# RWKV-7 attention and a cosine MoE on one core: r with v in block-diagonal products of two heads, memsets behind the first loads, and a new written order

## The chip, the core and the metric

The kernel runs on one core of a Trainium2 chip. The metric is the device time of one execution in microseconds. Before the change three runs gave 759.09, 759.76 and 762.46 us, a median of 759.76 us. A profiled execution of the same kernel took 755.39 us.

## The reference

The inputs r, k, v, w, a and b have the shape (4, 8, 768, 40): batch, heads, sequence, head size. The first part is a recurrence over the sequence with one 40x40 state for each of the 32 pairs of batch and head. The second part takes the result as 3072 tokens of 320 features through two weight matrices with a product with a cosine between them.

```python
for t in range(S):
    kt, vt, rt = (k[:, :, t], v[:, :, t], r[:, :, t])
    wt, at, bt = (w[:, :, t], a[:, :, t], b[:, :, t])
    y[:, :, t] = np.einsum('bhd,bhde->bhe', rt, state)
    Sa = np.einsum('bhde,bhe->bhd', state, at)
    state_decay = state * wt[:, :, None, :] - np.einsum('bhd,bhe->bhde', Sa, bt)
    state = state_decay + np.einsum('bhd,bhe->bhde', vt, kt)
...
h = x @ w_in
g = h * np.cos(h)
return (g @ w_out).astype(np.float32)
```

w_in is 320x2048 and w_out 2048x320; both arrive as 64-bit floats, which the kernel rounds to 32 bits by its own integer and float steps on VectorE and ScalarE.

## The kernel before

The sequence is cut into 24 chunks of 32 steps. Within a chunk the recurrence is solved with matrices: decays are multiplied up (w), a, b, k, r and v are brought into a layout with the features on the partitions, products between them give 32x32 matrices for each batch and head ("gram" is k with a and r with v; "nps" is b with a), a triangular inverse is computed on VectorE for four chunks at a time, and a chain of TensorE steps carries the state from chunk to chunk: t (turn the state), q (state with r), x, s, z. Every two chunks make a group of 256 tokens for the MoE: twelve groups, each in four parts j. A part is fa and fb (x with w_in, in the tile ph), y (cosine and product), then u, m, ms and c (the second product in the seven-product form; the first groups use the plain form sd).

The features of two heads (e = 0 and 1) lie in partitions 0 to 39 and 64 to 103; 40 to 63 and 104 to 127 are padding. A matrix product of one head therefore uses 40 rows of TensorE, and two heads use different halves of the rows. The output is 32 partitions for each of the four batches (blk, line 190).

The order of all instructions is a text, PLAN (line 17): 1536 tokens, which do() at line 532 executes one after the other; each engine, and each DMA queue, keeps that order for its own instructions. The tokens that are needed here:

- L:c:n:queue:part loads input n of chunk c (chunks 0 to 3), as two DMAs of 40 KB (load, line 256) from SyncE (s), ScalarE (a) or GpSimd (p). ld:c:n loads later chunks from SyncE.
- pw, pa, pb, pn (lines 538 to 637) make the turned w, a and b of two chunks and their products. pa calls over_w (line 563), whose reciprocal runs on VectorE and whose product bn on GpSimd reads nat_b; from_one (line 559) is a small memset of wb on GpSimd, and a_W (line 569) multiplies a by the decays on VectorE.
- sf, sc, ss (lines 344 to 367) fetch, multiply up and store w for later chunks; wf, wt, wm, wg, wp (line 413 on) round one piece of the weights; is, ip, ij, it, ih, ie, F and S make the inverse.
- in copies v and r of a chunk into vp and rp; v, k turn them with TensorE (chunks 0 to 7; from chunk 8 on r and v are turned through DRAM: rf, pt, st, and lt:c:n loads the turned tile, line 303).
- g is p2_g (line 759), with the two gram products; tk and tb take a chunk's result through DRAM into the MoE's input xT (line 938).
- B:n, K:n and P:n put n matmuls on the zero tile idle into TensorE's queue (lines 1150 to 1179).

Ahead of the plan stand constants and memsets: the identity (line 224), the mask su with its four selections (line 376), the paddings of seven tiles bn and two kn (lines 393 to 396), idle (line 406), all on GpSimd, and the paddings of w, a, vp and rp and the tile qz on VectorE (lines 239, 248, 254). Tiles that rotate through a pool ("ring" with 6 buffers, sb2 with 2) make a later writer wait for the last reader of the buffer.

## Time and profile before

| what | value |
| --- | --- |
| median of three runs | 759.76 us (759.09 to 762.46) |
| profiled execution | 755.39 us |
| its span, first to last instruction | 753.7 us |
| granted clock of TensorE, mean | 0.983 |
| TensorE busy | 702.8 us (93%), 17956 records |
| VectorE busy | 534.8 us (71%) |
| ScalarE busy | 398.0 us (53%) |
| GpSimd busy | 245.8 us (33%) |
| gram, k with a: records | 1536 of 40*32 by 32 columns |
| gram, r with v: records | 512 (chunks 0 to 7), 1024 (chunks 8 to 23) |

The profile comes from one execution. Times in the text that belong to a place count from the first instruction of that execution. PE is TensorE, DVE VectorE, ACT ScalarE, POOL GpSimd and SP SyncE. A line of the timeline holds start, length, engine, source line, operation, out<-in, the tile of TensorE (rows*columns), the shape of the moving data, and how many instructions are merged; in brackets stands the idle time ahead of it with the one that ended it. TensorE's instructions overlap, so their lengths do not add up; the distance from one start to the next does.

### The profile page before, as it was taken

To read this page: it belongs to the slowest core of one execution; us is meant where nothing else is said; L and a number is where in the kernel's file an instruction comes from. 1 tells how busy PE (TensorE), PEld (TensorE's weight loads), DVE (VectorE), ACT (ScalarE), POOL (GpSimd) and SP (SyncE) were. 2 spreads that over 40 slices of the span, in tenths; PEclk is the share of its full clock that TensorE was granted. 3 is DMA by queue.
4 is the path that set the end of the run, shared out by engine and by line. 5 is a ranking of instruction groups with operands and counts; after the bars stand their busy time and mean duration, and the time that the engine had idled before them with its cause. 6 is when DMAs were issued, how large, how long until landed. Compare 5 with 4: busy or idle time off the path is not lost.

```text
span 753.7 us, 40220 instructions
## 1 busy us (share of the span) xinstructions
PE 702.8 (93%) x17956; PEld 578.2 (77%) x17956; DVE 534.8 (71%) x1199; ACT 398.0 (53%) x764; POOL 245.8 (33%) x427
## 2 busy tenths in 40 slices
PE   4659899999999999989999999999999999999995
PEld 2546577777777777878888888888888788888885
DVE  7799888976467777568987758998367984534442
ACT  1335575775656665655645746546456444544442
POOL 8545304221241442450440442332242412321211
PEclk9779999999999999999999999999999999999998
DMA  7667455564565657655656667557543212110000
GB/s 118 130 168 183 149 152 136 116 132 75 117 119 113 123 107 145 130 130 115 139 118 110 128 130 155 107 118 120 102 78 76 62 41 59 48 29 13 21 18 17
DMA packets 267580, 78.11 MB, mean 104 GB/s; under 512 B 229104, under 2 KB 260848, under 8 KB 267408
## 3 DMA queue, kind: packets, MB, share of 16 engines
q1 hardware_dynamic: 264976, 73.66, 46.7%
q8 instruction: 141, 2.31, 1.3%
q0 software_dynamic: 1344, 1.72, 1.2%
q10 hardware_dynamic: 1088, 0.16, 0.1%
q14 instruction: 31, 0.25, 0.1%
HBM read 54.53 MB, written 20.97 MB: 100 GB/s over the span
## 4 chain that ended last, share of the span: by engine, by line
PE 69%; DVE 13%; ACT 5%; DMA 4%; SPq 4%; issue 3%; POOL 1%; DVEq 0%; POOLq 0%; ACTq 0%
PE ph L210 28%; PE po L210 17%; PE dps L210 4%; PE x0ps L210 4%; PE gram L210 3%; PE p L210 3%; SPq L262 2%; PE sps L210 2%; PE qps L210 2%; DVE inv L659 2%; PE nps L210 2%; DVE inv_tmp L655 2%; DVE gT L1010 2%; PE sT L807 1%; DMA nat_v<-in_v_dram 1%
## 5 line engine op out<-in xcount | busy, mean ns | idle before, releaser
L210 PE MATMUL ph<-xT,w_in_sb 128*128 128x256 f32 x768 | 184.3, 386 | 2.5 <-issue 1.0
L210 PEld LDWEIGHTS ph<-xT,w_in_sb 128*128 128x128 f32 x768 | 139.8, 190 | 31.1 <-issue 12.0
L210 PE MATMUL po<-w_out_sb,gT 128*128 128x160 f32 (+1 forms) x624 | 130.3, 347 | 3.0 <-DVE gT L1010 2.3
L1002 DVE SCALAR_TENSOR_TENSOR turns<-turns,ph 128x512 f32<-128x512 f32 x96 | 63.6, 685 | 93.5 <-ACT turns L1000 93.2
L1000 ACT ACTIVATE turns<-ph,few 128x512 f32<-128x512 f32 x96 | 63.6, 686 | 120.2 <-PE ph L210 110.1
L210 PEld LDWEIGHTS po<-w_out_sb,gT 128*128 128x128 f32 x624 | 97.1, 190 | 21.5 <-DVE gT L1010 3.3
L917 POOL TENSOR_TENSOR qz<-qz,wc 128x160 f32<-128x160 f32 x92 | 40.0, 457 | 132.5 <-DVE qz L916 132.5
L1010 DVE TENSOR_TENSOR gT<-ph,turns 128x512 f32<-128x512 f32 x96 | 64.4, 684 | 21.1 <-ACT turns L1007 20.8
L1007 ACT ACTIVATE turns<-turns,few 128x512 f32<-128x512 f32 x96 | 69.3, 722 | 3.1
L1006 ACT ACTIVATE turns<-turns 128x512 f32<-128x512 f32 x96 | 60.1, 626 | 12.4 <-DVE turns L1002 12.3
L1090 POOL TENSOR_TENSOR s<-gT 128x256 f32<-128x256 f32 x36 | 26.9, 747 | 97.3 <-DVE gT L1086 97.3
L210 PE MATMUL ph<-xT,w_in_tail 64*128 64x256 f32 (+1 forms) x464 | 54.5, 396 | 0.0
L291 ACT COPY nat_a<-ws 128x416 f32<-128x416 f32 (+1 forms) x45 | 45.1, 1019 | 16.9 <-DMA wdv<-nat_a 5.7
L210 PE MATMUL po<-TW,gT 128*128 128x160 f32 x288 | 51.4, 300 | 1.8 <-DVE gT L1086 1.2
L659 DVE TENSOR_TENSOR inv<-inv,inv_tmp 128x31 f32<-128x31 f32 (+15 forms) x124 | 50.0, 404 | 4.2
L1082 POOL TENSOR_TENSOR s<-gT 128x256 f32<-128x256 f32 x36 | 27.2, 757 | 78.7 <-DVE gT L1010 72.7
L825 ACT COPY qz<-qps 40x256 f32<-40x256 f32 x92 | 33.8, 367 | 30.8 <-PE qps L210 29.3
L655 DVE TENSOR_TENSOR inv_tmp<-u,inv 128x31 f32<-128x31 f32 (+15 forms) x124 | 46.5, 375 | 2.7
L566 POOL TENSOR_TENSOR bn<-nat_b,rw 128x320 f32<-128x320 f32 x22 | 19.3, 878 | 84.8 <-DVE rw L565 39.2
L210 PEld LDWEIGHTS po<-TW,gT 128*128 128x128 f32 x288 | 42.9, 190 | 2.8 <-DVE gT L1086 1.9
L565 DVE RECIPROCAL rw<-nat_w 128x320 f32<-128x320 f32 x20 | 42.6, 2139 | 0.0
L916 DVE TENSOR_TENSOR qz<-dps,qz 128x160 f32<-128x160 f32 x92 | 29.2, 317 | 16.8 <-PE dps L210 16.8
(158 smaller groups left out, 1248.5 us busy)
## 6 DMA issues: line engine op xcount, KB each, us to landing
words<-in_moe_w_in_dram SPq DMA_DIRECT2D x8, 512.0 KB
xd<-yt SPq DMA_DIRECT2D x48, 80.0 KB
out_dram<-ot SPq DMA_DIRECT2D x24, 160.0 KB
nat_v<-in_v_dram SPq DMA_DIRECT2D x90, 40.0 KB
nat_k<-in_k_dram SPq DMA_DIRECT2D x90, 40.0 KB
nat_b<-in_b_dram SPq DMA_DIRECT2D x84, 40.0 KB
wd<-ws SPq DMA_DIRECT2D x5, 640.0 KB
nat_w<-wd SPq DMA_DIRECT2D x80, 40.0 KB
```

The costliest lines, as they stand in the source:

```text
L210: nc.tensor.matmul(o, lhsT=lhsT, rhs=rhs, start=start, stop=stop, skip_group_check=True)
L291: nc.scalar.copy(quad_part(n, q, i).rearrange("p (d t) -> p d t", t=C), ws[:, :, PARTS[i]].rearrange("p t d -> p d t"))
L565: nc.vector.reciprocal(rw, wn)
L655: nc.vector.tensor_tensor(tmp, u[:, j : j + 1, :j].to_broadcast([P, C - j, j]), x[:, j:, j : j + 1].to_broadcast([P, C - j, j]), ALU.mult,)
L659: nc.vector.tensor_tensor(x[:, j:, :j], x[:, j:, :j], tmp, ALU.subtract)
L825: nc.scalar.copy(pick(qz[rows], f * (NZ - C), (NZ, 2 * B), (1, C)), ps[f][rows, : 2 * B * C].rearrange("p (i t) -> p i t", t=C),)
L917: nc.gpsimd.tensor_tensor(z, z, wc.rearrange("p (b f m) -> p f m b" if re_laid("w", c // 4) else "p (f m b) -> p f m b", f=2, m=2)[:, :, : ...
L1000: nc.scalar.activation(t, u, ACTF.Identity, bias=rnd, scale=1.0)
L1002: nc.vector.scalar_tensor_tensor(t, t, -ROUND, u, ALU.add, ALU.subtract)
L1006: nc.scalar.activation(t, t, ACTF.Abs)
L1007: nc.scalar.activation(t, t, ACTF.Sin, bias=half_pi, scale=-2.0 * math.pi)
L1010: nc.vector.tensor_tensor(gT[:, 2 * e : 2 * e + 2, :n], phs[e], ns[e].rearrange("p (f t) -> p f t", f=2), ALU.mult)
```

## The change

The change has three parts.

First, the product of r with v from chunk 8 on. r's tile gets two halves: the first holds head e = 0 in partitions 0 to 39 with zeros in 64 to 127, the second holds head e = 1 in 64 to 103 with zeros in 0 to 63. One matmul then takes v of both heads (104 rows) and 64 columns of r, and its two blocks of 32 columns are the products of the two heads. There are 16 such matmuls in a chunk in place of 32, and the results lie in the two banks by pairs of j instead of by head, so the copies and masks behind them read with other strides. The two r tiles are twice as large; the natural-order r and the tile rp live in their unused parts. The ring tile rw gets 5 buffers instead of 6. The empty halves are zeroed by GpSimd at the first two loads (chunks 8 and 9).

```diff
     def turned_load(c, n):
...
+            G[tag, c] = aT_b[c % 6] if n == "a" else next_r()
+            if n == "a":
+                to = G[tag, c].rearrange("p j t -> p (j t)")
+            elif n == "r" and not turned_r[r_used[-1]]:
+                turned_r[r_used[-1]] = True
+                for e in range(2):
+                    nc.gpsimd.memset(G["rT", c][full[1 - e], e], 0.0)
         for e in range(2):
+            if n == "r":
+                to = G["rT", c][:, e]
...
     def p2_g(c):
...
+        joined = re_laid("r", c // 4)
         for j in range(4):
             for bb in range(B):
+                if joined:
+                    o = (HH + 2 * (j % 2)) * C
+                    mm(
+                        ps[j // 2][blk[bb], o : o + 2 * C], piece("v", c, joint, j, bb),
+                        pick(G["rT", c][joint], bb * P + j * C, (4 * P, 2), (1, C)), False,
+                    )
+                    continue
                 for e in range(2):
                     mm(
```

Second, the front. The memset of idle is the first instruction of VectorE. The memsets of su, of bn and kn, and of vp, rp and qz become tokens of the plan (su, pk, qz), which stand behind the first loads. About half of the first loads change their queue: fifteen tokens go out from ScalarE, against two before.

```diff
+    idle = const.tile([P, P], BF16, tag="idle", name="idle")
+    nc.vector.memset(idle, 0.0)
...
+    def fill_padding():
+        for t in [*bn_b, *kn_b]:
+            nc.gpsimd.memset(padding(t), 0.0)
+        for i in (4, 5):
+            nc.gpsimd.memset(bn_b[i][:, :, C // 2 : C], 0.0)
...
-L:3:w:s:r pw:0 L:0:k:s:l L:2:a:p:r pa:0 L:3:b:p:r L:3:a:s:l sf:1 pw:2 B:4 L:2:b:p:l pa:2 wf:1 pb:0 sp:0 B:3
...
+L:0:w:a:r B:2 L:1:a:s:l L:1:a:s:r L:0:w:p:l L:1:w:a:l L:0:a:a:r B:4 B:5 L:3:b:s:l L:1:w:a:r L:0:b:p:l
+L:0:a:p:l pk L:2:a:s:l L:3:a:s:r L:3:w:s:r L:2:b:p:r L:2:w:p:r qz L:0:b:p:r L:3:w:a:l pw:0 B:3 L:2:w:a:l
+L:0:r:a:l L:2:a:s:r L:0:v:a:r L:1:b:p:l L:1:b:s:r pa:0 pw:2 L:0:k:a:r L:3:b:s:r L:0:k:p:l B:4 L:3:a:a:l su
+L:2:b:a:l sf:1 pa:2 wf:1 pb:0 pn:0 lo:0 sc:1 sp:0 ld:5:a pb:2 pn:2 L:0:r:p:r is:0 lo:2 L:0:v:s:l kn:0 in:0
```

Third, the order of the rest. Apart from the loads and the three new tokens, both plans hold the same tokens, the fillers included; their order differs from the first line to the last. Some places that the prediction speaks of:

```diff
-wt:12 wm:12 kn:3 K:4 wt:13 S:0:2:0 tb:0 wm:13 wg:13 wp:13 v:3 k:3 tb:1 fa:0:0 wg:12 wf:14 fb:0:0 ld:5:b wp:12
...
+tk:0 k:2 wf:5 s:1 v:2 K:14 wt:9 wm:9 wt:8 wg:9 wm:8 wp:9 g:2 wf:10 wt:10 tb:0 wm:10 wg:8 wp:8 B:6 z:1 B:6
+L:3:v:a:r wg:10 wp:10 t:2 wf:12 in:3 q:2 K:6 B:6 wf:11 wt:11 tk:1 wf:13 wt:5 B:3 wm:5 wg:11 wm:11 wp:11
+L:3:k:a:l tb:1 x:2 wt:13 wm:13 wg:5 wp:5 S:0:2:0 v:3 wt:12 K:4 wm:12 wg:13 wp:13 wf:14 fa:0:0 fb:0:0 y:0:0:1
...
+st:v:2:2 fa:2:0 ss:3 T:2:0 o:0:1 q:6 pt:w:3:0 st:w:3:0 lt:8:r ld:12:b fb:2:0 y:2:0:0 kn:7 ld:8:k x:6 lt:8:v
...
+s:18 fa:8:1 z:18 c:7:3 fb:8:1 o:7:0 lt:19:r u:8:0:1 g:19 ij:20:26 ij:20:25 m:8:0:0 u:8:0:2 y:8:1:0 y:8:1:2
```

## The prediction

> **What bounds the kernel now.** I read the page's slices first, because a mean over the span hides its stages.

> ```profile
> PE   4659899999999999989999999999999999999995
> DVE  7799888976467777568987758998367984534442
> PEclk9779999999999999999999999999999999999998
> DMA  7667455564565657655656667557543212110000
> ```

> A slice is 18.8 us. For the first five slices TensorE is half used and VectorE is the fuller engine; from about 97 us on TensorE is full. The stage sums put numbers to the second part: from 97 to 700 us, PE is busy 588.9 of 603 us at clock 1.00, and in the list of waits of PE after 97 us the largest entry is 2.3 us. So a microsecond of PE work saved or added there is a microsecond of time; shorter work elsewhere buys nothing there except out of some 14 us of idling.

> The start I read in the timelines of VectorE and GpSimd. Up to 24.8 us VectorE has no gap since 9.6 us; then comes the largest stall of the start:

> ```profile
> 22.68 2.15 DVE L565 RECIPROCAL rw<-wn 128x320 f32<-128x320 f32 x1
> 28.74 0.69 DVE L571 TENSOR_TENSOR aT<-aps,wb 128x512 f32<-128x512 f32 x1 [3.92 <-POOL wb L561]
> ```
> ```profile
> 20.38 1.16 POOL L262 DMA_DIRECT2D w_out_sb<-in_b_dram  x2
> ...
> 27.79 0.86 POOL L566 TENSOR_TENSOR bn<-w_out_sb,rw 128x320 f32<-128x320 f32 x1 [6.12 <-DMA w_out_sb<-in_b_dram]
> 28.58 0.12 POOL L561 MEMSET wb<- 128x16 f32 x1
> ```

> VectorE stands 3.92 us for a GpSimd memset that is queued behind a product, which waits for a load that GpSimd issued only at 20.38 us (chunk 2's b, kept in a part of w_out_sb). After this stall VectorE works 8.3 to 9.9 us of every 10 until 97 us: the start is VectorE's work plus its waits.

> TensorE's tiled runs I read in its timeline around gram 20:

> ```profile
> 599.35 1.07 PE L210 MATMUL ph<-xT,w_in_tail 64*64 64x256 f32 x16
> 600.35 1.99 PE L210 MATMUL ph<-xT,w_in_sb 128*128 128x256 f32 x8
> 602.28 0.72 PE L210 MATMUL gram<-aT,kT 40*32 40x32 f32 x62
> ...
> 602.84 0.73 PE L210 MATMUL gram<-rT,vp 40*32 40x32 f32 x62
> 603.50 0.66 PE L521 MATMUL kT<-ident,kn 128*128 128x128 f32 x4
> 603.99 1.25 PE L210 MATMUL po<-w_out_sb,gT 128*128 128x160 f32 x8
> ```

> Differences of the starts count here, since the durations overlap. Each program matmul leaves two records. The 64 records of k with a take 0.54 us (602.28 to about 602.82), 8.5 ns each; the 64 of r with v take 0.68 us to the next run. The same number in the same shape, but the second run ends in a change to the whole array: that change costs 0.14 us.

> **Part 1: r with v by two heads (chunks 8 to 23).** 32 matmuls of 40x32 by 32 columns (64 records) become 16 of 104x32 by 64 columns (32 records). Before, the pair of runs is 0.54 + 0.68 = 1.22 us. After, the first run also ends in a change of shape: 0.68 us. The new run has no row here; each of its matmuls takes all rows of one of four column strips, so four can be under way at once, where now eight can. The nearest row is the 64*64 tail run above, also four at once: 1.00 us for 16 records of 256 columns, less 0.14 for its change, is 0.86/16 = 54 ns per record, or 0.21 ns per column; 64 columns make 13.4 ns, 32 records 0.43 us, plus 0.14. Sum 0.68 + 0.57 = 1.25 us: 0.03 slower a chunk, +0.5 us in all. The other bound is that a record costs its 8.5 ns whatever its columns: 0.27 + 0.14 + 0.68 = 1.09, a gain of 0.13 a chunk, -2.1 us. The bound from above is a row that shares nothing: kT takes 0.49 us for 4 records of 128 columns, 0.96 ns per column, 61 ns for 64 columns, 1.96 us a run, +1.56 us a chunk, +25 us. I take the middle of the first two, **-0.8 us**, because four at once is what the tail run already shows.

> [...]

> The evacuations (two copies of 0.27 us on ScalarE, two masks of 0.28 us on VectorE a chunk) keep count and size, and only their strides change; the nearest row with such strides (masks of x, line 875, 0.28 to 0.29 us) says nothing is added. On GpSimd four memsets of r's empty halves come before loads 8 and 9. They wait for q of chunk 6 and 7, and SyncE's loads behind them wait too; the 128x1024 memset of inv takes 0.95 us, so each (64x512) is under 0.5 us, and GpSimd is busy only a third of the time there: nothing. If that cover failed, SyncE would be late by the memsets, about 1 us, once.

> **Part 2: memsets and loads.** Removed from the front: idle's memset moves from GpSimd at 5.06 us to VectorE's first place, and GpSimd's memsets of su, bn and kn (0.95 to 5.0 us) go behind its first loads, so its first load goes out near 1.8 us instead of 5.20 us. ScalarE takes 15 load tokens instead of 2, 11 of them ahead of 20 us (0.49 us an issue, 1.94 us for 4, on an engine busy 0.75 us between 5 and 20 us), GpSimd and SyncE fewer (0.58 and 0.48 us an issue). The first transposes wait today for GpSimd's w load (5.20 plus two issues plus about 2.8 us to landing: 8.5). With ScalarE's last w load issued by 4.2 to 5.5 us the start is at 7.0 to 8.3 us: **-0.8 us**. Chunk 2's b (left half) now goes out from ScalarE. It stands behind the copies of the second w pair, which wait for VectorE until about 16.8 us, and behind four issues of k and a; so it goes out at about 19 us, and ws and the first weight words (1.15 MB, issued at 16.05 and 16.78 us now, on queues whose busy share is 0.79 to 0.99 from 10 to 20 us) go out at about 12 us and are past. Landing in 3 to 6 us, 22 to 25 us, gives the memset at 23 to 26 us; VectorE is ready at 24.0. Of the stall, 0 to 2.0 us are left instead of 3.92: **-3.0 us** taken. What is then late next is VectorE's own work. If b lands as late as today, the -3.0 is nothing.

> **Part 3: the written order.** I counted the tokens ahead of landmarks in both lists. Ahead of the first MoE product (fa:0:0) both hold the same rounding, inverse and chain steps of VectorE, and k of chunk 3 moves behind it. xT's loads (tb:0) go ahead of three weight fetches instead of directly before tb:1; now tb:0 and tb:1 are issued back to back from 91.0 to 95.7 us and PE waits 0.6 us for xT at 96.7: **-0.6 us**. From there on I counted changes of TensorE's shape, token by token: 311 in either order, without the 16 of part 1. The idle fillers (B, K, P) are the same number. Of the chain steps that follow each other directly, some open (gram 19 and 21 had v's load right ahead) and some close (q and x of 21, s and z of 15, r's load before gram 19). PE's 14 us of idling from 97 to 700 us is what the order can win or lose: 0 taken, a third (4 us) either way.

> **Sum**, against the profiled execution (755.39 us, span 753.7): -0.8 - 0.8 - 3.0 - 0.6 = **-5.2 us**, 750.2. The shown runs have a median of 759.76, 4.4 above that execution; on it, **754.6 us**. Half a per cent, 3.8 us, is about what a measurement of this kernel can tell from no change.

> **The rivals.**
> 1. The stall stays: b lands as late, since more loads are in flight (for: queues 99% busy at 10 to 15 us; against: ws and the words go ahead). -5.2 + 3.0 + 0.8 gives -1.4: 758.4. Chance 0.18.
> 2. More is won: the products halve (-2.1 instead of -0.8), and a third of PE's idling goes (-4): -10.5, 749.3. For: gram's second run has gaps now, the longest 0.84 us at 332 us, and most of r's and v's loads move forward. Chance 0.16.
> 3. Slower: r's and v's turned loads come late to gram. This line of the chain of waits shows the size of one such load:

> ```profile
> 498.88 2.16 DMA vp<-wdv
> ```
> Behind it, gram 17 had to wait. r's load 8 now waits for GpSimd and PE, and load 19 stands right before its gram behind an output store. Each chunk that waits a full load loses 2.2 us; slower than no change from three chunks on, and five give +11 - 5.2 = +5.8: 765.6. Against: in most chunks 8 to 50 us of PE work lie between. Chance 0.12.
> 4. The four strips do not overlap: +25 - 4.4 = +20.6, 780; it makes the kernel slower from about 21 ns a record on (4.4/16 = 0.275 us more a chunk). Against it stands the tail run. Chance 0.04.

> The forecast has 0.50, with 751 to 758 as its own range. Faster by over 0.5% (below 756.0): 0.35 of it, all of rival 2, 0.01 of rival 1: 0.52. Slower: rivals 3 and 4: 0.16. Within: 0.32. The range takes in rival 2 and rival 3 and leaves out rival 4 and tails: 747 to 766.

> **What would show it.** Right: VectorE's stall before aT of chunk 3 under 2 us, and ws's scan starting at 25 to 27 us instead of 29.4; fa:0:0 at 91 to 93 us instead of 96.8; the gram pair at 1.09 to 1.25 us from first start to the next run; 256 matmuls (512 records) fewer; PE still over 97% busy from there on. Wrong: DMA named before gram or xT for more than 3 us in all; a new run of over 0.8 us; GpSimd waiting for b at 22 us again; fa:0:0 earlier, but the end not.

## The result, and the profile after

The changed kernel took 767.94 us (median of four runs, 767.27 to 768.42). The kernel before, run beside it, took 761.06 us. The ratio is 1.0092, with a 95% interval of 1.0062 to 1.0121: **slower by 7 us**, where 754.6 us was forecast with a range up to 766. The profiled execution took 767.68 us, its span is 765.7 us (before: 755.39 and 753.7). The profiled execution of before lies 5.7 us under the median beside it, that of after 0.3 us under its own, so the two traces differ by 12.3 us where the medians differ by 6.9. The kernel before was run again beside every experiment; its medians were 757.7 to 764.0 us, so a ratio below is always to the runs of before beside it.

The page's slices of the kernel after; a slice is 19.1 us:

```profile
PE   6767999999999999999999999999899999999995
DVE  6885989987446888568889668988557895454443
PEclk8578899999999999999999999999999999999999
DMA  9465565646555547466557667446751320300100
```

TensorE is full from the fifth slice on, as before. The difference is ahead of that: the granted clock is lower in the first five slices. The first product of the MoE, fa:0:0, starts at 103.1 us instead of 96.8. From there to TensorE's end it is 655.2 us instead of 649.8.

Two stalls of the start show what the change did there. The timeline of VectorE, where the 3.92 us stood before:

```profile
21.70 2.13 DVE L603 RECIPROCAL rw<-wn 128x320 f32<-128x320 f32 x1
25.11 0.69 DVE L609 TENSOR_TENSOR aT<-aps,wb 128x512 f32<-128x512 f32 x1 [1.29 <-POOL wb L599]
...
28.33 1.70 DVE L389 TENSOR_TENSOR ws<-ws 128x640 f32<-128x640 f32 x2
```

The wait is down to 1.29 us, yet ws's scan starts at 28.33 us, only 1.0 us earlier than before (29.35). The chain of waits names what was lost (start, length, what):

```profile
0.82 2.59 DMA nat_w<-in_w_dram
3.43 3.97 DMA nat_w<-in_w_dram
7.42 3.03 DMA nat_w<-in_w_dram
68.78 5.29 DMA words<-in_moe_w_out_dram
```

The first three lines are loads of w in a row: the last w half left ScalarE at 7.42 us, when the semaphore that it shares with an earlier load had come free (that load's last event on it is at 7.40 us). TensorE's timelines, after and before, show the transposes that wait for these loads: four came 2.1 us earlier than before, the other four 1.8 us later.

```profile
6.64 0.63 PE L559 MATMUL wT<-ident,nat_w 128*128 128x128 f32 x4 [0.97 <-DMA nat_w<-in_w_dram]
10.54 1.09 PE L559 MATMUL wT<-ident,nat_w 128*128 128x128 f32 x4 [3.27 <-DMA nat_w<-in_w_dram]
```
```profile
8.73 1.04 PE L521 MATMUL wT<-ident,nat_w 128*128 128x128 f32 x8
```

The fourth line of the chain is a new stop. The timelines of GpSimd, SyncE's queue, VectorE and TensorE around it:

```profile
65.61 1.31 POOL L779 TENSOR_TENSOR kn<-nat_k,rw 128x320 f32<-128x320 f32 x1
```
```profile
57.03 0.83 SPq L461 DMA_DIRECT2D words<-in_moe_w_in_dram  x2
66.94 0.82 SPq L278 DMA_DIRECT2D nat_k<-in_k_dram  x2
67.81 1.41 SPq L461 DMA_DIRECT2D words<-in_moe_w_out_dram  x3
```
```profile
67.78 0.68 DVE L476 SCALAR_TENSOR_TENSOR expo<-words,expo 128x512 int32<-128x512 int32 x1
74.15 0.43 DVE L469 TENSOR_SCALAR mant<-words 128x512 int32<-128x512 int32 x1 [5.70 <-DMA words<-in_moe_w_out_dram]
```
```profile
72.19 0.43 PE L212 MATMUL x0ps<-vvm,ag 32*32 32x72 f32 x18 [0.85 <-issue]
76.64 1.67 PE L212 MATMUL x0ps<-qz,aT 40*32 40x72 f32 x50 [4.01 <-ACT qz L884]
```

Nothing leaves SyncE for 9 us. At its head stands L:3:k:s:r, the load of k for chunk 3, which waits for the last reader of the buffer: kn of chunk 2, a product that GpSimd runs from 65.61 to 66.92 us. Behind it stands wf:4, three transfers of weight words. They land at 74.1 us; VectorE has no other work that may go ahead in its order and stands 5.70 us. TensorE stands 4.01 us behind that, for a copy of qz (76.24 us) that stands on ScalarE behind the rounding of the same words.

fa:0:0 itself starts at 103.08 us, after a wait of TensorE of 1.20 us. The profile names no releaser for it, but the semaphore of the load of xT for chunk 1 (tb:1, issued at 99.27 us) has its last event at 102.99 us. Before, TensorE waited 0.60 us for that load.

The gram pair of chunk 20 after, in TensorE's timeline:

```profile
612.75 0.76 PE L212 MATMUL gram<-aT,kT 40*32 40x32 f32 x64
613.44 0.65 PE L212 MATMUL gram<-rT,vp 104*32 104x64 f32 x32
614.02 0.66 PE L559 MATMUL kT<-ident,kn 128*128 128x128 f32 x4
```

From the first start to the next run 1.27 us (0.69 + 0.58) against 1.22 before, in this one of the 16 chunks.

### The profile page after: what moved, and what is told of

It reads as the page before. It is cut to its first block, busy times and chain, and to the rows that moved or that the text cites. A ratio compares the mean times of both kernels' runs of the same rounds, so it can differ in the third digit from the quotient of the medians.

```text
span 765.7 us, 39187 instructions
## 1 busy us (share of the span) xinstructions
PE 715.9 (94%) x17444; PEld 584.3 (76%) x17444; DVE 540.2 (71%) x1200; ACT 399.2 (52%) x764; POOL 242.4 (32%) x418
## 4 chain that ended last, share of the span: by engine, by line
PE 63%; DVE 18%; ACT 5%; SPq 4%; DMA 4%; issue 3%; POOL 2%; DVEq 0%; POOLq 0%; ACTq 0%
PE ph L212 23%; PE po L212 16%; PE dps L212 4%; PE x0ps L212 3%; DVE inv L697 3%; PE sps L212 2%; PE gram L212 2%; DVE inv_tmp L693 2%; SPq L278 2%; PE p L212 2%; DVE turns L1061 2%; PE qps L212 2%; PE nps L212 1%; DVE rw L603 1%; DMA nat_w<-in_w_dram 1%
## 5 line engine op out<-in xcount | busy, mean ns | idle before, releaser
L212 PEld LDWEIGHTS ph<-xT,w_in_sb 128*128 128x128 f32 x768 | 140.4, 191 | 34.8 <-issue 15.2
L212 PEld LDWEIGHTS po<-w_out_sb,gT 128*128 128x128 f32 x624 | 97.0, 190 | 21.3 <-issue 4.0
L1069 DVE TENSOR_TENSOR gT<-ph,turns 128x512 f32<-128x512 f32 x96 | 64.6, 685 | 20.6 <-ACT turns L1066 20.4
L307 ACT COPY nat_a<-ws 128x416 f32<-128x416 f32 (+1 forms) x45 | 46.1, 1023 | 21.3 <-DMA ws<-in_v_dram 6.8
L697 DVE TENSOR_TENSOR inv<-inv,inv_tmp 128x31 f32<-128x31 f32 (+15 forms) x124 | 53.5, 431 | 4.3
L1141 POOL TENSOR_TENSOR s<-gT 128x256 f32<-128x256 f32 x36 | 27.3, 759 | 83.1 <-DVE gT L1069 50.3
L693 DVE TENSOR_TENSOR inv_tmp<-u,inv 128x31 f32<-128x31 f32 (+15 forms) x124 | 48.2, 388 | 3.7 <-POOL inv L680 0.7
L884 ACT COPY qz<-qps 40x256 f32<-40x256 f32 x92 | 33.7, 366 | 28.8 <-PE qps L212 27.3
L212 PEld LDWEIGHTS ph<-xT,w_in_tail 64*128 64x128 f32 (+1 forms) x464 | 32.4, 170 | 11.1 <-issue 6.6
```

The lines of the kernel that those rows point to most:

```text
L212: nc.tensor.matmul(o, lhsT=lhsT, rhs=rhs, start=start, stop=stop, skip_group_check=True)
L307: nc.scalar.copy(quad_part(n, q, i).rearrange("p (d t) -> p d t", t=C), ws[:, :, PARTS[i]].rearrange("p t d -> p d t"))
L693: nc.vector.tensor_tensor(tmp, u[:, j : j + 1, :j].to_broadcast([P, C - j, j]), x[:, j:, j : j + 1].to_broadcast([P, C - j, j]), ALU.mult,)
L697: nc.vector.tensor_tensor(x[:, j:, :j], x[:, j:, :j], tmp, ALU.subtract)
L884: nc.scalar.copy(pick(qz[rows], f * (NZ - C), (NZ, 2 * B), (1, C)), ps[f][rows, : 2 * B * C].rearrange("p (i t) -> p i t", t=C),)
L1069: nc.vector.tensor_tensor(gT[:, 2 * e : 2 * e + 2, :n], phs[e], ns[e].rearrange("p (f t) -> p f t", f=2), ALU.mult)
```

## The experiments

**e1 to e4: parts of the order, the product alone.** My first theory was S: the loss is made at the start, by queues and wf:4, and the product is near zero. The rivals were the product, and the order of the rest.

e1 has the old order and queues up to fa:0:0 (the three memset tokens in front), then what is left of the new order.

```diff
-L:0:w:a:r B:2 L:1:a:s:l L:1:a:s:r L:0:w:p:l L:1:w:a:l L:0:a:a:r B:4 B:5 L:3:b:s:l L:1:w:a:r L:0:b:p:l
...
+su pk qz B:4 L:0:w:s:l L:3:w:s:l L:1:w:p:l L:1:w:a:r L:2:w:p:r L:0:a:s:l L:1:a:s:l L:1:a:s:r L:0:w:a:r
```

> The order and the load queues of the kernel before up to the first MoE product (fa:0:0), the order of the changed kernel from there on, with the two-head product; the three memset tokens stand at the very front. Theory (the start is most of the loss: fa:0:0 at 103.1 us in place of 96.8, and what follows is bound by TensorE): about 6 us below the changed kernel, 761 to 763 us, and fa:0:0 at 96 to 98 us. Rival A (the new order of the rest and the product are the loss, and the start is made up for later): 767 to 768 us.

764.20 us, 1.0034 [1.0010, 1.0059]; fa:0:0 at 99.6 us. The time lies between the theory's and the rival's: about 4 of the 7 us go with what stands ahead of fa:0:0.

e2 is the kernel after with r by single heads.

```diff
-        joined = re_laid("r", c // 4)
+        joined = False
```

> The changed kernel with r and v multiplied by single heads again (32 matmuls of 40x32 by 32 columns a chunk, from the same two-half r tile, memsets kept); order and loads as changed. Theory (the product costs 0.05 us a chunk, 1.27 against 1.22 us a gram pair in the traces, 0.8 us in all): 766 to 768 us, 0 to 2 us below the changed kernel. Rival B (the wide product holds back more than its own run, by its late results): 762 to 764 us.

790.18 us, 1.0386 [1.0321, 1.0452]. No theory allowed for this: 22 us more for a product that costs as much either way.

e3 moves one token of the new order.

```diff
-K:6 F:0:1:0 B:3 kn:2 L:3:k:s:r t:1 B:5 wf:4 wt:4
+K:6 F:0:1:0 B:3 kn:2 wf:4 L:3:k:s:r t:1 B:5 wt:4
```

> The changed kernel with one token moved: the weight fetch wf:4 goes ahead of the load L:3:k:s:r in SyncE's queue, which waits for GpSimd's last reader of k. Theory (VectorE's 5.7 us wait for that fetch at 68.5 us is on the path that sets the end): the wait goes, x of chunk 1 comes 4 to 6 us earlier, and the time is 762 to 765 us. Rival C (VectorE's next wait takes its place, or TensorE makes up for it before the end): the wait goes, but the time stays within 2 us of the changed kernel, 766 to 768 us.

VectorE's 5.70 us are gone, and s of chunk 1 follows its t after 11.2 us instead of 16.2; fa:0:0 comes at 100.5. But the time was 768.55 us, 1.0112 [1.0069, 1.0155]: no gain at the end.

e4 is the whole old order with the new product.

```diff
+        joined = re_laid("r", c // 4)
...
+su pk qz
 B:4 L:0:w:s:l L:3:w:s:l L:1:w:p:l L:1:w:a:r L:2:w:p:r L:0:a:s:l L:1:a:s:l L:1:a:s:r L:0:w:a:r L:3:a:s:r
```

> The kernel before in order and load queues, with the two-head product from chunk 8 on and its r tiles and ring sizes alone; the memset tokens at the very front. Theory (0.05 us a chunk): 0 to 2 us above the kernel before, 761 to 764 us. Rival B (the product is the loss): 766 to 768 us.

777.60 us, 1.0224 [1.0160, 1.0289]; again far from every theory. The old order is bad with the new product, the new order with the old one.

**Where e2 and e4 lose.** e4's timeline of TensorE, and its stretches (time, busy us of PE, PEld, DVE, ACT, POOL, then the clock, DMA share and GB/s):

```profile
459.80 1.05 PE L209 MATMUL nps<-aT,bT 40*32 40x32 f32 x90
460.78 0.57 PE L209 MATMUL qps<-rT,s 40*40 40x32 f32 x36
464.01 0.75 PE L209 MATMUL qps<-rT,s 40*40 40x32 f32 x28 [2.66 <-issue]
```
```profile
461.00:464.00 3.00, 0.35 (x35) 0.24 (x23) 2.08 (x3) 0.89 (x2) 0.00 (x0) 0.87 0.61 108
464.00:470.00 6.00, 5.99 (x43) 5.21 (x44) 5.52 (x15) 1.46 (x4) 1.54 (x2) 0.50 0.70 147
```

TensorE stops in the middle of a run, after 36 of 64 equal matmuls. "issue" means that nothing in the profile held it. Behind the stop the granted clock is 0.50. The page's list of DMA queues (this line is after's) has the hint, a queue that by its name, instruction, carries the program itself (packets, MB, share):

```profile
q8 instruction: 137, 2.24, 1.3%
```

Each packet is 16 KB. The packets follow the work, one for every 127 matmul records with their 127 weight loads (after: 137 packets, 17444 records; before: 141 and 17956); with TensorE's semaphore instructions, two a packet (286 in after, 280 in before), that makes about 256 instructions to a packet. Over all profiled executions TensorE stops 157 times for 0.6 us or more between 105 and 735 us. In 81 of them the first matmul behind the stop starts 1.2 to 1.8 us after such a packet has landed, in none 0.6 to 1.2 us after it; the other 76 are spread from 0 to over 6 us. In 73 of the 81 the profile names no releaser, of the others in 3. That gave **theory F**: a packet is asked for when TensorE enters a block and brings the next one; a block that is worked off in under about 3.8 us ends in a wait. Its first half, when a packet is asked for, is an assumption that no run here shows by itself; the 3.8 us is my estimate, and e12 below measured 3.57. Small tiles take 9 to 13 ns a record, 127 of them 1.1 to 1.7 us, and the large products of ph 216 ns (from start to start in before at 600 us), so by the theory a seam behind two runs of small tiles stalls, and one inside large products doesn't. I cut the traces at the seams and summed what blocks lack to 3.8 us: before 5 us, after 3 us, e4 18 us. The next four runs tested this.

e5 and e6 add matmuls of one row and one column to the kernel before, 24 or 127.

```diff
-K:29 y:0:0:2
+K:29 P:24 y:0:0:2
```

> The kernel before with 24 more 1x1 matmuls that do nothing, put behind the keepers that follow fa:0:0; nothing else differs. Theory F (TensorE's program comes in blocks of 256 instructions, one 16 KB transfer each; a block that is worked off in under about 3.8 us ends in a wait for the next one, and a wait of over some 1.2 us is followed by a piece of half clock): 24 matmuls move the seam between blocks by 24 matmuls everywhere behind them; from the trace of before, blocks cut at the new seams that last under 3.8 us add up to 29 us of waits instead of 5, in 25 places, 12 of them over 1.1 us. With some 2 us of lost clock for each of the 12 the time goes up by 40 to 50 us, to 800 to 812. Rival O (place in the program is without meaning; what counts is the order and the work): 24 matmuls of 26 ns are 0.6 us, so 761 to 763.

> The kernel before with 127 instead of 24 such matmuls at the same place. Theory F: 127 matmuls with their weight loads are one whole block (254 and two or so semaphore instructions), so the seams behind them fall where they fell before: waits of 5 us in all as before, no wait over 1.1 us, and the time goes up by the 127 x 26 ns = 3.3 us at most, 762 to 766; less than the 24 cost. Rival O: 3.3 us, and the 24 less than this.

e5, 24 more: 791.55 us, **1.0346 [1.0294, 1.0397]**. e6, 127 more: 766.07 us, **1.0026 [0.9998, 1.0053]**. By these ratios the 24 cost 26 us and the 127 cost 2. The two largest of PE's waits in e5 (us in all, times, longest):

```profile
PE qps L208 <- issue: 4.6, 2, 2.3
PE gram L208 <- issue: 4.3, 2, 3.0
```

The waits behind packets are 26.0 us (29 forecast), and 41 us run at half clock. That is 19 us of waits more than before and 20 us of lost clock (half of the 41), together about the 40 us by which e5's profiled execution is longer; the median rose by less, 27.6 us, under the forecast's 40 to 50.

e7 is e4 with 92 such matmuls where the cut trace wants them.

```diff
-t:7
+P:12 t:7
...
-s:11
+P:44 s:11
...
-q:21
+P:36 q:21
```

> The order of before with the two-head product, as in e4, and 92 1x1 matmuls in three places (12 ahead of t:7, 44 ahead of s:11, 36 ahead of q:21), found by cutting the trace of e4 at the seams that they give. Theory F: waits for blocks fall from 18 to 7 us, those over 1.1 us from 8 to 1 or 3, the half clock with them, and the 92 matmuls cost 2.4 us: 754 to 763, some 18 us under e4 although it has more work than e4. Rival P (the two-head product itself, or its turned copy of r, is what costs in e4): 778 to 782. Rival O (order against the product): the same, 778 to 782.

764.23 us, 0.9995 [0.9968, 1.0021]: **more work than e4 and 2.2% less time**, a little over the 754 to 763 expected. Its trace has 6.8 us at half clock where e4's has 30.7. So what e4 loses is its seams; with them moved, no cost of the product is left to measure.

e12 puts 1280 of them in a row. Its timeline:

```profile
106.14 5.41 PE L208 MATMUL pad<-idle 128*1 128x1 bf16 x211
112.21 10.25 PE L208 MATMUL pad<-idle 128*1 128x1 bf16 x384 [0.66 <-issue]
122.85 6.79 PE L208 MATMUL pad<-idle 128*1 128x1 bf16 x256 [0.39 <-issue]
130.03 6.79 PE L208 MATMUL pad<-idle 128*1 128x1 bf16 x256 [0.39 <-issue]
137.21 4.72 PE L208 MATMUL pad<-idle 128*1 128x1 bf16 x173 [0.39 <-issue]
```

> The kernel before with 1280 1x1 matmuls behind the keepers that follow fa:0:0, ten blocks of 128 with their 128 weight loads. Theory F: they are worked off faster than their blocks come, so TensorE stops after every 128th of them, each block takes 3.4 to 4 us whatever its 128 x 26 ns = 3.3 us, the ten take 35 to 40 us, and behind them the seams fall as in before (no wait over 1.2 us): 798 to 805. Rival (no such seams): 1280 x 26 ns = 33 us without a stop in them, 793 to 796.

A stop after every 128th matmul (the view merges those under 0.3 us): seven blocks from 112.21 to 137.21 are 3.57 us each, of which 128 x 25 ns = 3.2 us are work. The rival, no stops, falls; the floor is a little lower than I had put it. The time of the one execution, 793.62 us, lies below my 798 to 805 and in the rival's 793 to 796, so the verdict rests on the stops in the trace. All seven blocks ran at half the granted clock (110.4 to 148.0 us); whether the floor is the same at full clock isn't shown.

e17 does to after what e5 did to before.

```diff
-K:29
+K:29 P:24
```

> The kernel after with 24 more 1x1 matmuls at the keepers that follow fa:0:0, as e5 did to before. Theory F (the new order, too, stands well on its seams, and loses nothing to them against before): blocks under 3.8 us add up to 19 us of waits instead of 3, 9 of them over 1.1 us; with e5's lost clock for each the time goes up by 20 to 35 us, to 788 to 803. Rival (seams matter only to before's order): 768 to 770.

788.97 us in one execution; waits behind packets 13.6 us (19 forecast) instead of 4.1, half clock 27.3 us instead of 3.4. The new order, too, stands well on its seams. Behind 105 us after has 4.1 us of such waits and 3.4 us at half clock, before 7.2 and none, so the seams there are not the loss of the change. e2 was not run with padding, but its trace adds up: 15.2 us behind packets and 23.9 us at half clock are 11.1 us of waits and 10.2 us of lost clock more than in after, and its span is 21.4 us longer. So **the seams explain e4, shown by e7, and by this account e2, not the loss of the change**.

**e8 to e16: the start.** e8 is e3 with the last w half earlier.

```diff
-L:1:w:a:l L:0:a:a:r B:4 B:5 L:3:b:s:l L:1:w:a:r L:0:b:p:l
+L:1:w:a:l L:1:w:a:r L:0:a:a:r B:4 B:5 L:3:b:s:l L:0:b:p:l
```

> The kernel after with wf:4 ahead of the load of k for chunk 3 (as in e3) and the right half of chunk 1's w sent from ScalarE's queue right behind its left half, not behind a load of a. Theory S (a transfer of the hardware queues waits for the eighth-last one's landing, so the last w half left at 7.4 us): the second turned w starts at 7.5 to 8.5 us and not at 10.5, and fa:0:0 comes 1 to 2 us earlier than in e3 (98.5 to 99.5); the time 765 to 767 if nothing else moves. Rival (the first loads are hidden: chunk 0 waits for something else): fa:0:0 as in e3, 100.5, and the time 767 to 769.

The second w transposes start at 8.54 us, as forecast, but fa:0:0 at 102.5, no earlier than in e3. 764.54 us, 1.0035 [1.0002, 1.0069]. The late w is hidden.

e9 is the counterpart of e1: the new order up to fa:0:0, the old one behind, r by single heads.

```diff
-        joined = re_laid("r", c // 4)
+        joined = False
...
-wf:14 fa:0:0 fb:0:0 y:0:0:1 kn:3 sf:2 k:3 wg:12 ld:4:r
+wf:14 kn:3 k:3 fa:0:0 wg:12 fb:0:0 ld:5:b wp:12 y:0:0:0
```

> The new code with r by single heads; the new order up to fa:0:0 with its queues and memset places, and from there the order of before, so that seams between blocks of instructions fall about as in before. Theory S (some 4 us of the loss are made ahead of fa:0:0 and kept): fa:0:0 at 101 to 103.5 against 96.8 to 99.4 in three executions with the start of before; the time 764 to 768, 1.004 to 1.007 of before. Rival (what the start loses is made up later, the loss is in the order behind it): fa:0:0 late, but the time within 0.2% of before.

767.28 us, 1.0130 [1.0090, 1.0170]; fa:0:0 at 106.4. The cut itself added a stop of 3.25 us at kn of chunk 3, so the size is too large, but what the start loses is not made up later.

e10 is all of the change except product, order and queues.

```diff
-        joined = re_laid("r", c // 4)
+        joined = False
...
+su pk qz
 B:4 L:0:w:s:l L:3:w:s:l L:1:w:p:l L:1:w:a:r L:2:w:p:r L:0:a:s:l L:1:a:s:l L:1:a:s:r L:0:w:a:r L:3:a:s:r
```

> The new code with r by single heads and the whole order and queues of before, the three memset tokens in front: all of the change but product, order and queues (shared buffers, a bf16 idle tile filled by VectorE, five rw buffers). Theory S+F (none of these matters; the seams fall as in before): within 0.3% of before, fa:0:0 at 97 to 100, waits for blocks 4 to 8 us. Rival M (these edits, or the place of the memsets, cost what the start lost): 1.004 to 1.007 of before and fa:0:0 at 101 or later.

760.52 us, 1.0031 [1.0004, 1.0058]; fa:0:0 at 97.3. The waits behind packets were 10 us (7.2 in before) and 6.8 us ran at half clock (none in before); whether the seams moved here, and by what, was not shown. The start is that of before.

e11 is after with all 48 first loads on the old queues, 26 tokens changed, for instance:

```diff
-L:1:w:a:l L:0:a:a:r
+L:1:w:p:l L:0:a:s:r
```

> The kernel after with each of the 48 first loads on the queue that before has it on (26 change their queue), in the new order. Theory Q (the start loses by the queues: the loads taken off GpSimd's own queue stand in the ring of eight semaphores that SyncE and ScalarE share): fa:0:0 at 99 to 101 and the time 763 to 765. Rival O (the order of the instructions makes the start late, whatever the queue): fa:0:0 at 102 to 104 and the time 767 to 769.

766.55 us, 1.0111 [1.0061, 1.0162]; fa:0:0 at 104.0. The stop of wf:4 was gone (k went through GpSimd), but t of chunk 1 came at 72.4 us instead of 65.5. That is rival O's fa:0:0, but the run doesn't settle theory Q: right ahead of that t TensorE stood 3.79 us in the middle of a run of equal matmuls, up to 71.06 us and 1.4 us after a program packet had landed, and VectorE's wait for the wb memset was back with 4.2 us. What the queues alone are worth stays open.

e13 puts su pk qz in front of the new order; e14 does that together with the edits of e3 and e8; e15 puts them late in the old order of e10.

```diff
-L:0:w:a:r B:2 L:1:a:s:l
+su pk qz L:0:w:a:r B:2 L:1:a:s:l
```
```diff
-L:3:a:s:r L:0:b:p:r
+L:3:a:s:r pk L:0:b:p:r
...
-L:3:b:s:l L:1:b:s:r
+L:3:b:s:l qz L:1:b:s:r
...
-L:3:a:s:l sf:1
+L:3:a:s:l su sf:1
```

> The kernel after with its three memset tokens (the mask su, the paddings, qz) in front of all loads and the rest unchanged. Theory M (late memsets cost at the start: the mask's memset and four selections run on GpSimd at 23.3 to 24.9 us, ahead of the wb memset that VectorE's next aT waits for): fa:0:0 1 to 2 us earlier than the 103.1 to 103.4 of the new order, 101 to 102, and the time 1 to 2 us under after's, about 1.006 of before. Rival O (the order of TensorE's and SyncE's work makes the start late): fa:0:0 at 102.5 to 104 and 1.009 of before.

> The same with wf:4 ahead of the load of k for chunk 3 and the right half of chunk 1's w behind its left half, so all three named suspects of the start are undone in the new order. Theory M with S: fa:0:0 at 99 to 101 and the time 1.000 to 1.003 of before. Rival O (what is left of the new order is what is late): as e8, 1.0035 to 1.005 of before, fa:0:0 at 101 to 103.

> The new code with r by single heads and the order and queues of before, as e10, but the three memset tokens put behind the first loads, the paddings behind 10, qz behind 18, the mask ahead of sf:1, about where the new order has them. Theory M (late memsets cost): 1 to 2 us over e10, 1.005 of before, fa:0:0 at 98.5 to 100. Rival (they bring what they are for, first loads that leave earlier): 1 to 2 us under e10, fa:0:0 at 95 to 97, no slower than before.

e13: 769.27 us, 1.0093 [1.0063, 1.0123], fa:0:0 at 103.8. e14: 765.57 us, 1.0059 [1.0025, 1.0094], fa:0:0 at 99.8. e15: 762.87 us, 1.0024 [0.9998, 1.0050], fa:0:0 at 98.5. In time the place of the memsets can't be told from nothing, in either order: e13 is as after, e15 as e10, e14 no better than e8. Theory M falls, although e14's fa:0:0 came where it had it (99 to 101).

e16 puts the one stop into the old order of e10.

```diff
-wf:4 wp:3 wg:0 wp:0 B:4 L:2:k:s:r kn:2 B:3 K:14
+wp:3 wg:0 wp:0 B:4 L:2:k:s:r kn:2 L:3:k:s:r wf:4 B:3 K:14
```

The load's old token (L:3:k:p:r, on GpSimd's queue, 32 tokens further on) goes; the diff doesn't show it.

> The kernel of e10 (new code, r by single heads, order and queues of before) with the one stop of the new order put into it: the right half of chunk 3's k goes out from SyncE ahead of wf:4, directly behind kn:2, whose product on GpSimd it waits for. Theory W (this stop in SyncE's queue is half of what the new order loses ahead of fa:0:0): from the t of chunk 1 to its s 14 to 17 us instead of 10.4, VectorE idle some 5 us ahead of the rounding of wf:4, fa:0:0 at 99.5 to 102, and the time 2 to 4 us over e10's, 1.006 to 1.009 of before. Rival (VectorE catches it up before fa:0:0): t to s longer, fa:0:0 at 97 to 99 and the time as e10, 1.002 to 1.004.

765.74 us, **1.0102 [1.0070, 1.0134]**, against e10's 1.0031: 0.7%, 5 us. Its timelines of VectorE and of SyncE's queue show the same picture as after:

```profile
72.43 0.43 DVE L466 TENSOR_SCALAR mant<-words 128x512 int32<-128x512 int32 x1 [6.25 <-DMA words<-in_moe_w_out_dram]
```
```profile
65.65 0.81 SPq L275 DMA_DIRECT2D nat_k<-in_k_dram  x2
66.51 1.40 SPq L458 DMA_DIRECT2D words<-in_moe_w_out_dram  x3
```

fa:0:0 comes at 102.8 us against 97.3 in e10. Theory W holds for the start: these two tokens alone make fa:0:0 as late as in the new order. That the time follows is shown by the medians only. The profiled execution of e16 is its fastest (760.85 us) and no longer than e10's (761.80): behind fa:0:0 it has no half clock and 5.6 us of waits behind packets, e10's has 6.8 and 10.

**How far one fa:0:0 can be trusted.** TensorE stops behind program packets ahead of fa:0:0 too, for a different time in each of these runs: shortly ahead of t of chunk 1 it stands 0.68 us behind a packet in after, 1.96 in e3, 1.77 in e8 and 3.79 in e11. The kernel before, e5, e6 and e12 have the same tokens up to fa:0:0, and it starts at 96.8, 98.9, 99.4 and 99.0 us: a difference of 2 or 3 us between two single executions says little.

No version here beats the kernel before; e7 equals it. The intervals of e1, e7, e10 and e15 lie below that of after; those of e8 and e14 overlap it.

## Why the prediction was wrong

**Part 1 held.** 512 records went, as counted. The pair took 1.27 us; the worked 1.25 from the nearest row was closer than the middle that I took. Summed behind fa:0:0 from start to start, gaps over 0.1 us left out, the two gram runs take 27.75 us in e8 instead of 28.31 in before (neither has half clock there): -0.6 us against -0.8, so chunk 20 is not the mean. The strips overlapped as assumed: in chunk 20 the 32 records start within 435 ns, 14 ns apart (61 ns by the row of kT, which shares nothing), in groups of four, a group every 56 ns; and the next run follows 150 ns after the last one, so the change of shape costs 0.14 us there. The eight at once that I gave the old run are not shown: its records in before's gram 20, from 602.84 us, start in pairs, 16 or 17 ns from one pair to the next.

**Part 2 was right about the stall and wrong about its worth.** The stall fell from 3.92 to 1.29 us. Of the -3.0 us only 1.0 was left at ws's scan, since half of the first w was transposed 1.8 us later instead of 0.8 earlier; the reciprocals that need it start at 21.70 us instead of 20.09. The last w half, to be issued by 4.2 to 5.5 us, left at 7.42: I had read the number of transfers per engine, and not that SyncE's and ScalarE's transfers take their semaphores in turn from the same eight (100, 102, 113 to 118 in the trace), so that each waits for the eighth-last one's landing: ScalarE's last three loads of w left at 3.43, 5.36 and 7.42 us, 0.02 us after the last event of the load ahead of each on its semaphore. But neither shows at fa:0:0: with w early (e8) or with the memsets moved (e13, e15) it came no earlier than without. The -0.6 us of part 3 was not won either, since the load that TensorE waits for there is that of tb:1, and the wait grew from 0.60 to 1.20 us.

**The step that failed is "0 taken, a third (4 us) either way" of part 3, with its "ahead of the first MoE product both hold the same rounding, inverse and chain steps".** Counting tokens ahead of a landmark says nothing about what stands ahead of a transfer in its queue. I named k of chunk 3 as moved, but not its load, which came from GpSimd's queue to SyncE's, ahead of wf:4, with a wait for kn of chunk 2. fa:0:0 was forecast at 91 to 93 and came at 103.1: 11 of the 17 us by which the profiled execution missed its forecast (750.2). In nine executions with the old order it is at 96.8 to 100.6 (median 99.0), in four with the new one 103.1 to 104.0, and at 106.4 in e9; in three with the stop taken out of the new order 99.8 to 102.5, in e11, which lacks the stop as well, 104.0 behind its 3.79 us, and in e16, the stop in the old order, 102.8. By these single executions the stop is worth between 0.6 us of the start (e8 against after) and 5.5 (e16 against e10). The rest of the start's loss goes with the order (t of chunk 1 comes 0 to 3 us later) and was not taken apart. That the start is most of the loss is shown by e1: with the old one the time is 4 us less, although e1 has as much half clock behind 105 us as after (3.4 us) and more waits behind packets (5.9 us against 4.1).

**Behind fa:0:0 the new order loses some too, by the traces.** From fa:0:0 to TensorE's end it is 649.8 us in before and 649.3 in e16, with the old order, and 652.2 in e8, with the new one; none of the three has half clock there. In the time this is not shown: e1, which has only that part of the new order, is 2.6 us slower than before, but e10, with the old order throughout, is 2.4 us slower. The sums from start to start, e8 against before, put +1.0 us on sps, +0.9 on dps, +0.8 on kT (some 0.5 of it for chunk 3, whose k moved behind fa:0:0), +0.5 each on nps and x0ps, less 0.6 for gram and 1.1 for gaps over 0.1 us. Which neighbours cause it was not tested. Part 3's count of changes of shape, 311 in either order, gave no sign of it.

So e1 divides the 7 us into some 4 ahead of fa:0:0 and 2.6 behind it, and the second part has no run that explains it. What also stays open is the end of e3: the stop was gone and fa:0:0 earlier, and the time was not; its profile has 6.8 us at half clock behind 105 us where after has 3.4, one of the two pieces behind no wait over 0.6 us. e8 and e14, with the same edit and more, came out at 1.0035 and 1.0059. So putting the stop in cost time (e16), and taking it out alone did not give it back.

**The rivals.** Rival 3 had the right kind, a load that waits in a queue, in the wrong place: r's and v's turned loads cost nothing visible. Rival 1's stall did not stay.

## What to carry to other kernels

Where an order is written by hand, follow each DMA queue by itself: for every transfer that moves, write down what it waits for and what now stands behind it; here two tokens, a load ahead of a weight fetch, made the first product of the MoE 5.5 us late and the kernel 0.7% slower (e16 against e10). The places where TensorE's program is cut into blocks belong to this kernel, with its runs of 9 to 13 ns a record: 24 matmuls that do nothing cost 26 us (e5), 127 at the same place, about one block, cost 2 (e6). Where a kernel shows such seams, test a part of a change alone only with the seams kept (add or take away whole blocks, or a few idle matmuls), or the test measures the seams.

## What the runs showed of the hardware

The clock: in the records half clock comes in pieces of 3.41 us and multiples (in after 3.41 to 17.07 us, one of 3.41 behind 105 us). Between 105 and 735 us of all profiled executions, half clock set in during or within 5 us after all 15 waits of TensorE of 2.0 us or more, 9 of 22 between 1.3 and 2.0 us, 15 of 38 between 1.0 and 1.3, and 2 of 82 between 0.6 and 1.0. Counted as half its length, a piece of 3.41 or 6.83 us is 1.7 or 3.4 us of lost clock; so counted, waits and lost clock account for 39 of the 40 us by which e5's profiled execution is longer than before's, and for 21.3 of the 21.4 us by which e2's span is longer than after's. Not every piece follows a wait: 5 of the 44 come with no wait of 0.6 us or more, two of these in runs of one-column matmuls (e6 at 108.9 us, e12 from 110.4 us for 37.5 us).
